# A drain on GpSimd at the start of every slot of two expert layers

## The chip, the cores and the metric

The kernel runs on one core of a Trainium2 chip. The metric is the device time of one launch in microseconds (us); the median of three runs before the change is 854.3 us (853.04 to 856.71). The core's engines are named as in the profile: PE (TensorE matmul) and PEld (its weight loads), DVE (VectorE), ACT (ScalarE), POOL (GpSimd) and SP (SyncE). A name with a q behind it (POOLq, SPq) is the engine's own instruction queue: its waits, branches, register moves and drains, which the page does not count as busy.

## The reference

Three stages follow each other: a retention attention, a top-1 expert layer, and a second top-1 expert layer whose output is gated.

```python
# attention: 4 batches, 8 heads, 768 steps, head size 64
state = gamma * state + outer(k[t], v[t])
y[t] = scale * q[t] @ state
# layer 1: x is (3072, 512), 8 experts, F = 1024
logits = x @ w_gate + modality_bias[modality_id]
e = argmax(logits); gate = softmax(logits)[e]
x = gate * (relu(x @ w1[e]) @ w2[e])
# layer 2: the same with its own weights, and one more factor
out = gate * sigmoid(x @ w_output_gate)[e] * (relu(x @ w1[e]) @ w2[e])
```

## The kernel before

The attention runs over 24 units of 128 rows. As soon as a unit's rows have their expert and their place, GpSimd writes them to a scratch tensor in HBM, sorted by expert, with an indirect DMA (`scatter`, L469: one DMA for 128 rows). 24 such DMAs carry layer 1's input (`x1d`). Each expert layer then works on *slots* of 256 rows of one expert: rows are fetched by plain DMAs from SP's queue, transposed and split in two parts by DVE and ACT, multiplied with the expert's weights on PE (three products for each, since weights and activations are split into a high and a low part), and given their gate. A slot that holds at most 128 rows takes a smaller path (`run_small`); a branch on a count decides at run time. Layer 1's slots scatter their result, one slot later, to the second scratch tensor (`x2d`, L469 again, two DMAs for a slot); layer 2's slots scatter straight to the output (`done`, L919, two DMAs for a full slot and one for a small one).

Every slot begins with `ids`: on GpSimd a handful of tiny operations on 128 by 1 or 128 by 2 elements, which mark rows that don't belong to the slot (L845 to L859). In layer 1 they make `valid` and `invalid` (L852, L854) and copy the row numbers into the output tile (L856); DVE reads them when the slot's rows are routed, in the middle of the next slot. In layer 2 they make `to` (L858, L859), the row numbers that the slot's own output DMAs use.

In layer 1's first slot GpSimd has more to do: it makes two of the four low parts of the second weight matrix (`w2l`, L511, 128 by 1024 elements each) right behind `ids`, and behind them issues the last two of the 24 scatters. In layer 2's first slot it makes two as well.

The order within an engine is that of the program; each engine runs its own list and waits for others by semaphores alone. Where two branches meet, the one that issued fewer of GpSimd's DMAs raises those DMAs' semaphores by an instruction on GpSimd's queue (INC_SWDGE_SEM in the trace), so that both sides leave the same counts. At the end of the program every engine drains and all meet at a barrier; those instructions carry the line of the launch, L1202.

Of the kernel before, what the change touches and what calls it, by code (L numbers as in the profile page):

```python
# [416 lines left out]
def retention_moe_moe_kernel(ctx: ExitStack, tc: tile.TileContext, q, k, v, mod, mb, wg, wg2, w1, w2, cst_d, out):  # L417
    nc = tc.nc
# [184 lines left out]
    with ExitStack() as actx:  # L603
# [114 lines left out]
        for t0, t1 in groups:  # L718
            g, ids = group1(t0, t1, misc)
            late.setdefault(t1, []).append(g["choose"])  # L720
            early.setdefault(t1 + 1, []).append(g["rank"])
            late.setdefault(t1 + 1, []).append(g["place"])
            late.setdefault(t1 + 1, []).append(lambda g=g, ids=ids: seq([g["weigh"], lambda: once(ids)]))
            for t in range(t0, t1):
                written.setdefault(t + 6 if t < n - 12 else t1 + 2 + (t - t0) // 2 if t < n - 8 else n - 2 + (t - n + 8) // 3, []).append(t)
# [4 lines left out]
        for i in range(n):  # L730
# [52 lines left out]
            if i == n - 4:  # L783
                fetch_rows(x1d, first_row(rp1), 2, xqf, xmf, after=scattered[-4:] + blanks)
        g1, ids = group1(n - 2, n, misc)
        ids()


    with ExitStack() as mctx:
# [28 lines left out]
        class Slot:  # L818
# [20 lines left out]
                return fetch_rows(self.src, at, 2, self.xq, self.xm, cond, after, full, **kw)  # L839

            def ids(self, full=True):

                ts = slice(self.t0, self.t0 + 2)
                if not full:
                    nc.gpsimd.memset(invalid[:, ts][:, 0:1], float(2 * E * APART))  # L845
                    if self.li == 1:
                        nc.gpsimd.memset(valid[:, ts][:, 0:1], 0.0)
                for h in range(not full, 2):
                    t = slice(self.t0 + h, self.t0 + h + 1)
                    at = self.xm[:, h, R_BIG:R_BIG + 1]  # L850
                    pl = cst[:, C_PH + h:C_PH + h + 1]
                    nc.gpsimd.tensor_scalar(invalid[:, t], at, pl, float(2 * E * APART), op0=ALU.is_gt, op1=ALU.mult)  # L852
                    if self.li == 1:
                        nc.gpsimd.tensor_scalar(valid[:, t], at, pl, None, op0=ALU.is_le)  # L854
                if self.li == 1:
                    nc.gpsimd.tensor_copy(self.o[:, :, DM + R_ID], self.xm[:, :, R_ID])  # L856
                else:
                    nc.gpsimd.tensor_tensor(invalid[:, ts], invalid[:, ts], self.xm[:, :, R_ID], op=ALU.add)  # L858
                    nc.gpsimd.tensor_copy(to[:, ts], invalid[:, ts])  # L859
# [347 lines left out]
```

## Time and profile before

| what | us |
|---|---|
| median of three runs | 854.3 |
| the profiled execution's own time | 853.39 |
| its span, from the first to the last instruction | 851.5 |
| PE busy | 799.0 |
| DVE busy | 430.3 |
| ACT busy | 276.2 |
| POOL busy | 202.1 |

Busy time counts the engines' data instructions. The profiled execution took 1.9 us more than its span (launch and end, which no instruction covers). The page's chain of waits follows data instructions back from the last one, so it begins and ends with work; what the queues do after the last data instruction stands in the views of a line's instructions, which give for every kind the count, the least, median and greatest duration in ns, and the first and last start.

### The profile page before, as it was taken

Reading aid. Unit: us, or ns where it says so; the run is one execution under the profiler, and the core shown is the slowest. Engines: PE = TensorE matmul, PEld = TensorE weight load, DVE = VectorE, ACT = ScalarE, POOL = GpSimd, SP = SyncE. Lnnn points to the kernel's source line nnn. Section 1 sums busy time; section 2 is a strip of 40 time slices with the busy share of each in tenths; the row PEclk is TensorE's granted clock in tenths of the full one; section 3 lists DMA queues with packets and bytes.
Section 4 is the critical chain, followed back from the end, with each engine's and each line's share of the span. In section 5 each row is a group of like instructions: output and inputs, shape, how many; then the busy total and the mean of one; then the engine's idle time right before and its main releaser. Section 6 shows DMA issues by size and latency. Waiting matters only on the chain. (4 is left out here: it accounts for less than half of the span.)

```text
span 851.5 us, 18413 instructions
## 1 busy us (share of the span) xinstructions
PE 799.0 (94%) x5987; PEld 696.2 (82%) x5987; DVE 430.3 (51%) x1110; ACT 276.2 (32%) x476; POOL 202.1 (24%) x291
## 2 busy tenths in 40 slices
PE   8999998799999998999999787999999999999992
PEld 7888877788889977888899576997889888888871
DVE  4554556744444338334454676144555673545921
ACT  3444445312122124121222451113252551514610
POOL 3455456712221011222210032011211112020210
PEclk9999999899999999999999999999999999999997
DMA  9987799272111015311222523412726385252610
GB/s 163 236 224 185 177 240 305 99 253 72 40 40 51 15 53 162 116 53 51 58 71 52 177 76 121 157 40 54 251 65 209 100 285 172 94 173 70 207 40 16
DMA packets 149688, 106.98 MB, mean 126 GB/s; under 512 B 94845, under 2 KB 125693, under 8 KB 149504
## 3 DMA queue, kind: packets, MB, share of 16 engines
q1 hardware_dynamic: 141664, 85.37, 37.2%
q0 software_dynamic: 6400, 18.98, 6.0%
q8 instruction: 73, 1.20, 0.6%
q14 instruction: 111, 0.91, 0.4%
q10 hardware_dynamic: 1440, 0.53, 0.3%
HBM read 167.64 MB, written 25.83 MB: 227 GB/s over the span
## 5 line engine op out<-in xcount | busy, mean ns | idle before, releaser
L891 PE MATMUL hT<-xh,w1h 128*128 128x256 f32 x768 | 222.4, 290 | 4.7 <-issue 2.9
L891 PE MATMUL hT<-xl,w1h 128*128 128x256 f32 x768 | 216.7, 282 | 1.4 <-DVE xl L547 1.4
L891 PE MATMUL hT<-xh,w1l 128*128 128x256 f32 x768 | 216.5, 282 | 0.0
L909 PE MATMUL po<-w2h,hh 128*128 128x512 f32 x432 | 172.6, 400 | 0.3
L909 PE MATMUL po<-w2l,hh 128*128 128x512 f32 x432 | 171.2, 396 | 0.0
L891 PEld LDWEIGHTS hT<-xh,w1h 128*128 128x128 f32 x768 | 146.4, 191 | 12.4 <-issue 11.0
L891 PEld LDWEIGHTS hT<-xl,w1h 128*128 128x128 f32 x768 | 146.6, 191 | 2.9 <-DVE xl L547 2.2
L891 PEld LDWEIGHTS hT<-xh,w1l 128*128 128x128 f32 x768 | 146.4, 191 | 0.0
L909 PE MATMUL po<-w2h,hl 128*128 128x512 f32 x432 | 136.3, 396 | 0.5 <-DVE hl L904 0.5
L883 DVE SCALAR_TENSOR_TENSOR hl<-hT,hh 128x512 fp32r<-128x512 f32 x96 | 65.5, 689 | 136.3 <-ACT hh L882 105.8
L882 ACT ACTIVATE hh<-hT 128x512 fp32r<-128x512 f32 x96 | 57.0, 596 | 201.7 <-PE hT L891 191.9
L909 PEld LDWEIGHTS po<-w2h,hl 128*128 128x128 f32 x432 | 81.1, 188 | 21.8 <-DVE hl L904 2.0
L909 PEld LDWEIGHTS po<-w2h,hh 128*128 128x128 f32 x432 | 81.6, 189 | 19.6 <-ACT hh L903 1.6
L909 PEld LDWEIGHTS po<-w2l,hh 128*128 128x128 f32 x432 | 81.6, 189 | 18.0
L469 POOL DMA_INDIRECT x2d<-ob,r_idx x28 | 29.6, 1059 | 261.0 <-DVE ob L260 174.5
L919 POOL DMA_INDIRECT out_dram<-ob,to x28 | 30.2, 1079 | 217.4 <-DVE ob L917 139.8
L545 ACT ACTIVATE xh<-xTb 128x512 fp32r<-128x512 f32 x58 | 33.5, 624 | 88.5 <-DVE xTb L540 79.7
L511 DVE TENSOR_TENSOR w2l<-raw,w2h 128x1024 fp32r<-128x1024 f32 x40 | 47.3, 1234 | 13.7 <-DMA xqb<-x1d 6.2
L506 DVE TENSOR_TENSOR w1l<-raw,w1h 128x512 fp32r<-128x512 f32 x80 | 49.8, 683 | 2.5 <-ACT w1h L505 2.5
L547 DVE TENSOR_TENSOR xl<-xTb,xh 128x512 fp32r<-128x512 f32 x58 | 37.6, 690 | 22.3 <-ACT xh L545 22.3
L505 ACT ACTIVATE w1h<-raw 128x512 fp32r<-128x512 f32 (+1 forms) x84 | 47.7, 640 | 0.0
L915 DVE TENSOR_SCALAR ob<-po,xmb 128x512 f32<-128x512 f32 x24 | 18.0, 750 | 54.5 <-PE po L909 54.5
(205 smaller groups left out, 997.9 us busy)
## 6 DMA issues: line engine op xcount, KB each, us to landing
raw<-in_w_dram SPq DMA_DIRECT2D x248, 512.0 KB
xqb<-x2d SPq DMA_DIRECT2D x124, 64.0 KB
xqb<-x1d SPq DMA_DIRECT2D x108, 64.0 KB
nq<-in_q_dram SPq DMA_DIRECT2D x24, 256.0 KB
nk<-in_k_dram SPq DMA_DIRECT2D x24, 256.0 KB
nv<-in_v_dram SPq DMA_DIRECT2D x24, 256.0 KB
x1d<-zrow SPq DMA_DIRECT2D x4, 516.0 KB
x2d<-zrow SPq DMA_DIRECT2D x4, 516.0 KB
```

The lines of the kernel that those rows point to most:

```text
L469: return nc.gpsimd.indirect_dma_start(out=dst, out_offset=bass.IndirectOffsetOnAxis(ap=rp.idx[:, t:t + 1], axis=0), in_=row, in_offset=Non ...
L505: nc.scalar.activation(w1h[i][:, cols], raw1[i][:, cols], AF.Copy)
L506: los[i].tensor_tensor(w1l[i][:, cols], raw1[i][:, cols], w1h[i][:, cols], op=ALU.subtract)
L511: los[i].tensor_tensor(w2l[i], raw2[i], w2h[i], op=ALU.subtract)
L545: nc.scalar.activation(hi[:, k:k + 2, :], xT[:, k:k + 2, :], AF.Copy)
L547: nc.vector.tensor_tensor(lo[:, k:k + 2, :], xT[:, k:k + 2, :], hi[:, k:k + 2, :], op=ALU.subtract)
L882: nc.scalar.activation(hh[b], hT[b], AF.Relu)
L883: nc.vector.scalar_tensor_tensor(hl[b], in0=hT[b], scalar=0.0, in1=hh[b], op0=ALU.max, op1=ALU.subtract)
L891: nc.tensor.matmul(to, lhsT=a[k][:, fs], rhs=b[:, k, :], start=(k == 0 and m == 0), stop=(k == KD - 1 and m == 2))
L909: nc.tensor.matmul(po[h], lhsT=x[b][:, o:o + P], rhs=w[f // 2][:, f % 2, :], start=(f == 0 and i == 0), stop=(f == KF - 1 and x is hl))
L915: nc.vector.tensor_scalar(perm(o[:, :DM]), plain(po[h]), gate, None, op0=ALU.mult)
L919: nc.gpsimd.indirect_dma_start(out=out, out_offset=bass.IndirectOffsetOnAxis(ap=to[:, t:t + 1], axis=0), in_=o[:, :DM], in_offset=None, bo ...
```

## The change

`ids` gets a first line: an explicit drain on GpSimd. The operations behind it, their order and the waits of all engines stay as they were; on PE, ACT, SP and POOL the two programs have the same instructions in the same order but for the drains themselves (on DVE only numbers in the names of temporary tiles differ). The built program has 81 more drains on GpSimd, since both sides of every branch hold one; an execution meets one for each slot that it runs.

```diff
             def ids(self, full=True):
+                nc.gpsimd.drain()
 
                 ts = slice(self.t0, self.t0 + 2)
                 if not full:
```

## Rows read from the trace of the kernel before

**Rows 1.** The page: the span, and busy time, share of the span and instructions of two engines.

```profile
span 851.5 us, 18413 instructions
PE 799.0 (94%) x5987; PEld 696.2 (82%) x5987; DVE 430.3 (51%) x1110; ACT 276.2 (32%) x476; POOL 202.1 (24%) x291
```

**Rows 2.** Stretches of time: start and end, length, then for each engine busy us and instructions, the granted TensorE clock, the DMA share and GB/s. The last 13 us.

```profile
core 0: us, PE busy (x) PEld busy (x) DVE busy (x) ACT busy (x) POOL busy (x), PEclk, DMA share, GB/s
838.50:851.50 13.00, 0.00 (x0) 0.00 (x0) 0.00 (x0) 0.00 (x0) 0.01 (x1) 0.54 0.06 21
```

**Rows 3.** The instructions of L1202 (the program's end) from 843 us to 850.8 us, and then the drains behind them: count, duration in ns least/median/greatest, first and last start.

```profile
L1202 SPq EVENT_SEMAPHORE  x12: 28/28/28, 843.8 to 844.5; - x12
L1202 SPq DRAIN  x2: 7/10/13, 844.6 to 844.7; - x2
L1202 POOLq DRAIN  x1: 6610/6610/6610, 844.1 to 844.1; - x1
...
L1202 POOLq DRAIN  x2: 46/78/111, 850.9 to 851.2; - x2
L1202 ACTq DRAIN  x1: 8/8/8, 850.9 to 850.9; - x1
```

**Rows 4.** The instructions of L1194 (the program's beginning) on GpSimd's queue, the same columns.

```profile
L1194 POOLq INC_SWDGE_SEM  x1: 31/31/31, 0.1 to 0.1; - x1
L1194 POOLq DRAIN  x1: 171/171/171, 0.3 to 0.3; - x1
```

**Rows 5.** Four of the later INC_SWDGE_SEM on GpSimd's queue, in order of time, from the views of the lines L1136, L1086 and L1164, the same columns.

```profile
L1136 POOLq INC_SWDGE_SEM  x1: 1272/1272/1272, 534.2 to 534.2; - x1
...
L1086 POOLq INC_SWDGE_SEM  x1: 1337/1337/1337, 597.6 to 597.6; - x1
...
L1086 POOLq INC_SWDGE_SEM  x1: 1746/1746/1746, 837.2 to 837.2; - x1
...
L1164 POOLq INC_SWDGE_SEM  x1: 1767/1767/1767, 842.1 to 842.1; - x1
```

**Rows 6.** GpSimd's groups of instructions by line and tile: count, busy us, mean ns of one, idle time before and what ended it; and for the DMAs to the output, then to `x1d`, the time from issue to landing, least/median/greatest.

```profile
L919 POOL DMA_INDIRECT out_dram<-ob,to x28 | 30.2, 1079 | 217.4 <-DVE ob L917 139.8 <-DVE hl L883 18.3 <-issue 18.1
L469 POOL DMA_INDIRECT x2d<-ob,r_idx x28 | 29.6, 1059 | 261.0 <-DVE ob L260 174.5 <-DVE w1l L506 40.7 <-issue 22.1
L469 POOL DMA_INDIRECT x1d<-yn,r_idx x24 | 24.9, 1037 | 14.6 <-DVE P L655 3.6 <-DVE r_meta L334 3.2 <-ACT yn L578 3.0
L859 POOL CAST to<-invalid 128x2 uint32<-128x2 f32 x16 | 3.0, 187 | 1.1
L856 POOL COPY ob<-xmb 128x2 f32<-128x2 f32 x13 | 2.4, 186 | 7.8 <-DMA x2d<-ob,r_idx 5.0 <-issue 2.7
L856 POOL COPY ob<-xmf 128x2 f32<-128x2 f32 x1 | 0.2, 179 | 0.0
...
DMA to landing us min/median/max: 2.7/2.9/3.1
...
DMA to landing us min/median/max: 2.8/4.5/6.0
```

**Rows 7.** GpSimd in order of time (start, us, line, operation, tiles, count, in brackets the idle time before and its releaser): a full slot of layer 1; `w2l` in layer 2's first slot; and the least idle time behind `ids` of any slot, in layer 2.

```profile
224.67 0.97 POOL L469 DMA_INDIRECT x2d<-ob,r_idx  x1 [0.30 <-issue]
225.68 0.32 POOL L852 TENSOR_SCALAR invalid<-xmb,cst 128x1 f32<-128x1 f32 x1
...
227.82 0.18 POOL L856 COPY ob<-xmb 128x2 f32<-128x2 f32 x1
247.98 1.08 POOL L469 DMA_INDIRECT x2d<-ob,r_idx  x1 [19.98 <-DVE ob L260]
...
507.04 5.80 POOL L511 TENSOR_TENSOR w2l<-raw,w2h 128x1024 fp32r<-128x1024 f32 x2 [9.07 <-ACT w2h L510]
...
793.17 1.30 POOL L919 DMA_INDIRECT out_dram<-ob,to  x1 [6.37 <-DVE hl L904]
...
796.48 0.19 POOL L859 CAST to<-invalid 128x2 uint32<-128x2 f32 x1
802.33 0.10 POOL L1066 MEMSET ob<- 128x1 f32 x1 [5.66 <-DVE ob L1064]
```

**Rows 8.** All engines in order of time, layer 1's first slot: GpSimd, and the choice of experts for the attention's last rows (DVE L190 to L207, PE L215), the columns as in rows 7; and the three runs of L190 from 130 us to 170 us, the columns as in rows 3.

```profile
161.50 4.67 POOL L511 TENSOR_TENSOR w2l<-raw,w2h 128x1024 fp32r<-128x1024 f32 x2
161.63 4.57 DVE L190 TENSOR_TENSOR rdz<-r_lg,rmx 128x16 f32<-128x16 f32 x1
166.65 0.17 DVE L207 TENSOR_TENSOR r_oh<-rq,rm 128x16 bf16<-128x16 f32 x1
166.87 0.17 PE L215 MATMUL misc<-r_oh,cb 128*128 128x16 bf16 x1 [3.98 <-DVE r_oh L207]
...
169.38 1.08 POOL L469 DMA_INDIRECT x1d<-yn,r_idx  x1 [3.22 <-DVE r_meta L334]
...
L190 DVE TENSOR_TENSOR rdz<-r_lg,rmx x3: 192/2066/4569, 134.1 to 161.6; 128x16 f32<-128x16 f32 x2, 128x32 f32<-128x32 f32 x1
```

**Rows 9.** The stretch behind PE's wait of rows 8, columns as in rows 2; and in order of time the second slot's input getting ready on DVE and PE's first weight load of that slot.

```profile
167.10:170.50 3.40, 3.40 (x17) 3.40 (x18) 2.86 (x25) 0.60 (x1) 1.08 (x1) 0.50 0.00 0
...
182.12 1.29 DVE L547 TENSOR_TENSOR xl<-xTb,xh 128x512 fp32r<-128x512 f32 x2 [0.77 <-ACT xh L545]
...
183.78 0.19 PEld L891 LDWEIGHTS hT<-xh,w1h 128*128 128x128 f32 x1
```

## The prediction

> **What bounds the kernel now.** I read the page first: PE is busy for 799.0 of 851.5 us, GpSimd for 202.1 [rows 1]. Nothing that GpSimd does inside a slot should set the time, and a change to GpSimd alone would be worth nothing were the page the whole story. It is not, for busy time leaves out the queues. The view of stretches shows 13 us at the end in which no engine works on data [rows 2], and the instructions of the program's last line say what fills half of it: a drain on GpSimd that begins at 844.1 and takes 6.610 us, after which the barrier opens at once (850.7) and the program is over at 851.5 [rows 3]. On ACT a drain takes 8 ns, on SP 7 to 13. The chain of waits doesn't show this, since it ends at the last data instruction. So the tail is set by GpSimd's queue, and that is the place that I price.
>
> **What that drain waits for.** The last output DMA was issued at about 837.4 and such DMAs land 2.7 to 3.1 us after issue [rows 6], so by 840.5, while the drain starts at 844.1. It isn't waiting for that data. Three rows say that it works off a backlog of GpSimd's DMAs. The drain at the program's beginning, with none issued yet, took 0.171 us; the two behind the long one, with nothing issued in between, took 0.111 and 0.046 us [rows 3, 4]. And INC_SWDGE_SEM, which handles the same DMAs' semaphores, grows through the run: 0.031 us with none issued, 1.272 at 534.2 us, 1.337 at 597.6, 1.746 at 837.2 and 1.767 at 842.1 [rows 4, 5]. The DMAs issued by then, counted along the time line, are 54, 58, 79 and 80 (24 + 28 + 28 in all [rows 6]): (1.767 - 1.272) / (80 - 54) = 0.019 us for each, and the two values between lie on that line within 0.02 us. Something is kept for every DMA ever issued, and no instruction before the end clears it. By that the long drain pays 6.610 / 80 = 0.083 us for each.
>
> Here a page speaks against the change: the Trainium skill, "VectorE: DVE Perf Modes", section "The DRAIN you can't avoid", says of the drains ahead of and behind a program that they are a constant 12 ns or so on all five engines. By it the added drains would cost nothing and save nothing, and the time would stay at 854.3. The rows of ACT and SP agree with it (7 to 13 ns); GpSimd's 6610 ns doesn't, and the measurement decides.
>
> **The change, part by part.** One drain is added to each slot that runs: 14 in layer 1 (13 + 1 of L856) and 16 in layer 2 (L859), 30 in all [rows 6]. Each follows the last DMA of the slot before, and what is queued behind it is `ids`.
>
> *A drain inside a slot.* Its cost is not shown before; the rows bound it by 0.046 us (nothing to do) and 6.61 us (the longest). By the backlog reading it has two DMAs to work off, 2 x 0.083 = 0.17 us, and waits until they have landed: issued at 224.67, landed 2.7 to 3.1 us later, thus about 2 us beyond 225.68, where `ids` begins now [rows 7]. I take 2.2 us. Behind `ids` GpSimd is idle for 20 us in a full slot of layer 1, and for 5.66 us in the tightest slot [rows 7]; nothing but GpSimd's own DMA (layer 2) or the next slot's routing (layer 1) waits for `ids`. So 29 of the 30 cost nothing. In layer 2's first slot it is hidden too, for `w2l` there waits 9.07 us for ACT [rows 7].
>
> *Layer 1's first slot.* Here `ids` is followed at once by `w2l`, 4.67 us on GpSimd from 161.50. DVE's L190, a 0.19 us operation elsewhere, began at 161.63 and took 4.57 us: it was held until both `w2l` were done, and PE stood still for 3.98 us behind it and then ran at the 1.2 GHz level (granted clock 0.50) for 3.4 us [rows 8, 9]. The page "SBUF — State Buffer" of the Trainium skill, section "SBUF: two separate sides", calls this an exclusive lock that goes to whichever of DVE and GpSimd starts first; the row agrees. The drain has 22 DMAs behind it (all but the last two of 24), 22 x 0.083 = 1.8 us, and moves `w2l` to about 162.4. DVE's chain from L190 to L207 needs 0.8 us undisturbed (0.6 us from the end of L190 at 166.20 to that of L207 at 166.82, and its own 0.19), so it would be through at about 162.4 as well: a toss-up. If it is through, PE is 4 us ahead, but the second slot's input hangs on DVE's place chain, which still waits for `w2l` to end, and xl is ready only 0.4 us before PE needs it now (183.41 against 183.78 [rows 9]). So PE's lead can't be used beyond about 1.3 us, and another stop and another 3.4 us at half clock (1.7 us) may eat it. If it isn't through, everything is 0.9 us later. Between -1.3 and +0.9, I take +0.3 us.
>
> *The end.* The last slot is small and issues one DMA, so the last drain finds one: 0.171 + 0.083, some 0.2 us. What is late next is SP: its 12 waits run from 843.8, when GpSimd's last INC_SWDGE_SEM is over, to 844.7 [rows 3], so the barrier can't open before about 0.85 us after that instruction; then 0.8 us as now. The end from there on is 1.65 us instead of 851.5 - 843.87 = 7.63: -5.98 us. The INC_SWDGE_SEM of 1.767 us falls to what is left without a backlog, 1.767 - 80 x 0.019 = 0.25: -1.5 us. The one at 837.2 (1.746 us) does so too, but beside the DMA of 837.4, so I count half of 1.4: -0.7 us, with both ends, 0 and -1.4, kept for the range.
>
> Sum: -5.98 - 1.5 - 0.7 + 0.3 = -7.9 us. The profiled execution took 853.39, so 845.5 us by it; the median of the runs is 0.9 us above it, and the changed kernel's time is a median too: 854.3 - 7.9 = 846.4 us.
>
> **The rivals.**
>
> *The drain clears the backlog, but INC_SWDGE_SEM counts every DMA ever issued.* For it: its growth is the only thing measured, not its fall. Then 5.98 alone is saved: 854.3 - 5.98 + 0.3 = 848.6 us.
>
> *The slots' drains clear nothing for the end* (the change doesn't do what it says): the 6.6 us are a step of the end itself, or every drain walks through all DMAs so far. For it: only one long drain was seen. Against it: 0.111 and 0.046 us right behind it. The time is 854.3 + 0.3, up to 855.2 with the first slot's 0.9.
>
> *A fixed price for any drain that finds a DMA, about 6.6 us.* Then the end keeps its drain, and the first slot pays: `w2l` ends at 161.50 + 6.6 + 4.67 = 172.8, the scatter behind it goes from 169.38 to 172.8, past its 3.22 us of idle time, the second slot's input comes 3.4 us later, 2.9 of which PE feels, and standing still that long costs 3.4 us at half clock again: 2.9 + 1.7 = 4.6, so 858.9 us, slower than before. It decides from 3.2 us of drain in this slot on. Against it: the growth of INC_SWDGE_SEM by the count.
>
> **How the numbers follow.** The forecast has a chance of 0.63, the half gain 0.12, no gain 0.16, the fixed price 0.09. What a measurement can tell from no change is 0.5%, 4.3 us. The forecast's own range goes from 854.3 - 8.6 - 1.3 = 844.4 (the whole of the 1.4, the first slot at its best) to 848.1 (none of it, the first slot at +0.9, 0.4 us for runs). Together with the half gain that holds some 7 in 10; to have 8 it reaches over the case without gain: 844.0 to 855.2. Faster by over 0.5%: 0.75, the first two cases; within 0.5%: 0.17; slower: 0.08.
>
> **What would show it.** Right: GpSimd's drain at the end under 0.5 us; 30 drains on its queue in the slots, about 2 us each, the first near 1.8; the INC_SWDGE_SEM late in the run under 0.4 us; about 5 us in place of 13 behind the last data instruction; PE's sum of waits as before but for layer 1's first slot. Wrong: a drain of several us left at the end, or slots whose PE idle time grows behind `ids`.

## The result and the profile after

The changed kernel takes 841.91 us (median of 4 runs, 840.37 to 843.6); the kernel before took 854.96 beside it (4 runs, 853.04 to 856.71). The ratio is 0.9845, with a 95% interval of 0.9816 to 0.9874: about 13 us faster. The predicted time was 846.4 us, and the measured one lies below the predicted range. Two later timings of the changed kernel, called `again` and `again_b` below, gave 0.9849 and 0.9842.

The page after, the lines that answer to [rows 1]:

```profile
span 839.4 us, 18443 instructions
PE 796.4 (95%) x5987; PEld 691.8 (82%) x5987; DVE 430.2 (51%) x1110; ACT 276.4 (33%) x476; POOL 192.5 (23%) x291
```

There are 30 instructions more, one drain for each slot, and 12.1 us less of span. PE's busy time has fallen by 2.6 us only. Most of the gain is time in which PE did nothing, and it lies in two places.

**The end.** The end of the program on the queues of GpSimd and SP from 834 us on, which answers to [rows 3] (columns as there; L1203 is the line of the end now, since one line was added). Behind it the last two INC_SWDGE_SEM, which answer to the last two of [rows 5]:

```profile
L1203 SPq EVENT_SEMAPHORE  x14: 17/28/1795, 836.0 to 839.4; - x14
L1203 POOLq DRAIN  x3: 50/111/381, 837.7 to 839.2; - x3
...
L1087 POOLq INC_SWDGE_SEM  x1: 170/170/170, 834.8 to 834.8; - x1
...
L1165 POOLq INC_SWDGE_SEM  x1: 172/172/172, 835.9 to 835.9; - x1
```

The greatest drain at the end is 0.381 us where it was 6.610, and the semaphore instructions fell from 1.746 and 1.767 to 0.170 and 0.172. What is late now is SP: one of its waits takes 1.795 us. It ends when the last output DMA has landed, as far as the profiles show: here the landing is not recorded, in `again` it is (issued at 832.27 us, landed at 835.26), and SP's wait there ends at 835.29. Before the change the landing came long before the drain was over. The stretch from PE's last product to the end, in the view of stretches (columns as in [rows 2]), before and then after:

```profile
834.79:851.50 16.71, 0.00 (x0) 0.00 (x0) 1.24 (x3) 0.00 (x0) 1.18 (x2) 0.64 0.06 19
```

```profile
832.36:839.40 7.04, 0.00 (x1) 0.00 (x0) 1.24 (x3) 0.00 (x0) 1.18 (x2) 0.77 0.13 46
```

The work of DVE and POOL in it is the same to the hundredth (1.24 and 1.18 us), and the stretch is 9.7 us shorter.

**Layer 1's first slot.** All engines in order of time after the change, where [rows 8] stood. GpSimd first, then DVE:

```profile
163.75 0.18 POOL L857 COPY ob<-xmf 128x2 f32<-128x2 f32 x1
163.90 4.75 POOL L511 TENSOR_TENSOR w2l<-raw,w2h 128x1024 fp32r<-128x1024 f32 x2
170.03 1.08 POOL L469 DMA_INDIRECT x1d<-yn,r_idx  x1 [1.38 <-DVE r_meta L334]
```

```profile
163.19 0.18 DVE L190 TENSOR_TENSOR rdz<-r_lg,rmx 128x16 f32<-128x16 f32 x1
...
163.82 0.17 DVE L207 TENSOR_TENSOR r_oh<-rq,rm 128x16 bf16<-128x16 f32 x1
...
164.95 1.38 DVE L222 COPY r_base<-rR 128x8 f32<-128x8 f32 x1
166.24 2.45 DVE L227 TENSOR_TENSOR rR<-rR,r_oh 128x16 f32<-128x16 f32 x1
```

L190 takes its 0.18 us again, L207 has begun 0.08 us before `w2l` begins, and PE has its input. The two `w2l` now hold two later operations of DVE, L222 and L227, for which PE doesn't wait at once. The view of PE's waits, before and then after (total us, times, longest):

```profile
PE misc L215 <- DVE r_oh L207: 6.0, 2, 4.0
```

```profile
PE misc L215 <- DVE r_oh L207: 2.1, 1, 2.1
```

The wait of 4.0 us is gone, and with it the half clock behind it: the stretch of [rows 9] reads so now, with a granted clock of 1.00 in place of 0.50.

```profile
167.10:170.50 3.40, 3.40 (x23) 3.08 (x23) 3.37 (x22) 0.60 (x1) 2.02 (x2) 1.00 0.02 5
```

**Elsewhere.** From one full slot of layer 1 to the next PE needs 24.75 us before (208.70 to 233.45) and 24.74 after (207.21 to 231.95), with a drain in each. Two stretches did move. Layer 1's second slot is 0.7 us longer, 25.43 us (181.78 to 207.21) against 24.69 (184.01 to 208.70), because PE now waits for input between its first two products. The first two slots of layer 2 together are 2.3 us shorter, 53.89 against 56.24; kernels without a drain there have nearly the same (`delay` 54.30, `noport` 54.50), so this isn't put down to the drains. What is left of the span, without layer 1's first two slots and the end, is 779.5 us before and 779.8 after, and lies between 776.5 and 781.5 in the twelve profiled executions below.

### The profile page after: what moved, and what is told of

It reads as the page before. It is cut to its first block, busy times and chain, and to the rows that moved or that the text cites. A ratio compares the mean times of both kernels' runs of the same rounds, so it can differ in the third digit from the quotient of the medians.

```text
span 839.4 us, 18443 instructions
## 1 busy us (share of the span) xinstructions
PE 796.4 (95%) x5987; PEld 691.8 (82%) x5987; DVE 430.2 (51%) x1110; ACT 276.4 (33%) x476; POOL 192.5 (23%) x291
## 5 line engine op out<-in xcount | busy, mean ns | idle before, releaser
L511 DVE TENSOR_TENSOR w2l<-raw,w2h 128x1024 fp32r<-128x1024 f32 x40 | 47.3, 1233 | 14.2 <-DMA xqb<-x1d 6.7
L540 DVE STREAM_TRANSPOSE xTb<-xqb 128x1024 f32<-128x1024 f32 x29 | 36.0, 1242 | 24.4 <-DMA xmb<-x2d 13.4
```

Source lines behind the costliest of these rows:

```text
L511: los[i].tensor_tensor(w2l[i], raw2[i], w2h[i], op=ALU.subtract)
L540: nc.vector.transpose(xT.rearrange("p k (a i) -> p a k i", i=32), xq.rearrange("p a (k i) -> p a k i", k=KD))
```

## The experiments

Two quantities are compared below. The *slot* is the time on PE from the first product of layer 1's first slot to the first product of the second slot. The *tail* is the time from the end of PE's last product to the end of the span. Both come from each kernel's one profiled execution; the ratios come from the timings. The kernel before had a median of 853.57 us beside the first four runs, 855.18 beside the next four and 854.67 beside the last two.

| kernel | slot | tail | ratio, 95% interval |
|---|---|---|---|
| before | 30.61 | 16.73 | 1 |
| after | 27.17 | 7.07 | 0.9845 (0.9816 to 0.9874) |
| late | 31.17 | 7.07 | 0.9891 (0.9849 to 0.9932) |
| first1 | 27.26 | 13.01 | 0.9921 (0.9897 to 0.9945) |
| first2 | 31.85 | 8.36 | 0.9905 (0.9870 to 0.9940) |
| delay | 28.62 | 14.89 | 0.9951 (0.9927 to 0.9975) |
| noport | 25.94 | 16.40 | 0.9944 (0.9920 to 0.9967) |
| again | 27.41 | 7.09 | 0.9849 (0.9823 to 0.9876) |
| dvew2l | 25.69 | 7.10 | 0.9811 (0.9774 to 0.9847) |
| dveall | 25.65 | 7.53 | 0.9829 (0.9803 to 0.9855) |
| dvew2l_b | 25.68 | 6.92 | 0.9831 (0.9791 to 0.9872) |
| again_b | 27.28 | 6.92 | 0.9842 (0.9801 to 0.9883) |

Where the first slot is short, the second gives some of it back: it takes 24.7 us in `before`, `late` and `first2`, and 25.1 to 25.5 in the nine others.

My theory after the result: two gains that have nothing to do with each other, the cleared backlog at the end and the moved `w2l` in layer 1's first slot. The rival: all of it is the backlog, and the first slot's difference is chance.

**`late`: drains only in layer 2, from its third slot on.** The first slot keeps its old order, while the end finds everything cleared.

```diff
             def ids(self, full=True):
+                if self.li == 2 and self.i >= 2:
+                    nc.gpsimd.drain()
```

> Drains only in layer 2 from its third slot on. Backlog theory: the first of these drains finds some 56 DMAs and works them off in GpSimd's idle time (56 x 0.083 = 4.6 us on its queue), the drain at the end falls to about 0.4 us and the tail behind PE's last matmul from 16.7 to about 7.0 us; nothing changes before the third slot of layer 2, so the time falls by 9.7 us alone, ratio about 0.9887. Rival, the rest of the 13 us comes with the tail as well: ratio 0.985 as with all drains. Rival, a drain clears only what was issued in its own slot: end drain near 6 us, ratio 1.00.

Measured 0.9891, which is 9.3 us. The first slot is as before: DVE is held again, this time two operations by one `w2l` each (columns as in [rows 7]), and PE waits 3.62 us behind them. The tail is 7.07 us.

```profile
163.88 4.67 POOL L511 TENSOR_TENSOR w2l<-raw,w2h 128x1024 fp32r<-128x1024 f32 x2
...
164.17 2.11 DVE L190 TENSOR_TENSOR rdz<-r_lg,rmx 128x16 f32<-128x16 f32 x1
...
169.05 0.17 PE L215 MATMUL misc<-r_oh,cb 128*128 128x16 bf16 x1 [3.62 <-DVE r_oh L207]
```

So some 9 us belong to the end alone, and they don't need a drain in every slot. The interval reaches down to 0.9849, so this time by itself doesn't exclude that the end is the whole gain; the slot in the profile and the runs that follow do. The drain at the end takes 1.815 us here and not the 0.4 that was expected: it begins 1.2 us after the last DMA's issue (838.14 against 836.92) and is over 0.05 us behind SP's wait (839.96 against 839.91). The first of the drains in the slots finds 56 DMAs (columns as in [rows 3]):

```profile
L843 POOLq DRAIN  x1: 4650/4650/4650, 564.9 to 564.9; - x1
```

**`first1`: one drain, in layer 1's first slot.**

```diff
+                if self.li == 1 and self.first:
+                    nc.gpsimd.drain()
```

> A drain only in layer 1's first slot. Backlog theory: 22 DMAs are off the list, so the drain at the end takes (80 - 22) x 0.083 = 4.8 us in place of 6.61, the last INC_SWDGE_SEM 1.767 - 22 x 0.019 = 1.35; tail 16.7 - 2.6 = 14 us. With the port theory (w2l moved behind DVE's choice of experts) the slot itself is some 3.4 us shorter on PE: together 5 to 6 us, ratio 0.993. If the 3.4 us are drift between executions: ratio 0.997.

Measured 0.9921, 6.7 us. The slot is as short as in the changed kernel (27.26). The end keeps a backlog of 58 DMAs, since the drain cleared 22 of the 80.

**`first2`: one drain, in layer 2's first slot.**

```diff
+                if self.li == 2 and self.first:
+                    nc.gpsimd.drain()
```

> A drain only in layer 2's first slot. Backlog theory: it finds 50 DMAs and takes about 50 x 0.083 = 4.2 us or a little more (landing of the last two); 30 are left for the end: 30 x 0.083 = 2.5 us, the last INC_SWDGE_SEM 0.2 + 30 x 0.019 = 0.8; the tail falls by 4.1 + 1 to 2 us. If the 4 us that this slot was shorter on PE with all drains belong to the drain, they show here too (ratio 0.989); if they are drift of instruction fetch or clock, ratio about 0.993.

Measured 0.9905, 8.1 us; the slot is as before (31.85, with a wait of 4.26 us). The drain cleared 50 DMAs, and 30 are left. It took 5.911 us, of which 50 x 0.083 are 4.15; the last packets of the DMAs ahead of it moved until 3.3 us into it. In the profiles layer 2's first slot was 4 us shorter after the change (28.26 us) than before (32.23); with a drain there it takes 28.07 to 31.07 us in seven kernels, without one 28.22 to 32.23 in five, so that difference isn't the drain's. The drains at the end and the last INC_SWDGE_SEM of `first1`, then of `first2` (columns as in [rows 3]):

```profile
L1204 POOLq DRAIN  x3: 56/111/4810, 838.0 to 843.4; - x3
...
L1166 POOLq INC_SWDGE_SEM  x1: 1317/1317/1317, 836.5 to 836.5; - x1
```

```profile
L1204 POOLq DRAIN  x3: 52/111/2507, 841.7 to 844.7; - x3
...
L1166 POOLq INC_SWDGE_SEM  x1: 752/752/752, 840.7 to 840.7; - x1
```

With the kernel before and `late` that makes four points for the drain: 6.610 us for 80 DMAs, 4.810 for 58, 4.650 for 56, 2.507 for 30, that is 0.083 or 0.084 us for each. The last INC_SWDGE_SEM goes from 1.767 to 1.317 and 0.752: (1.767 - 0.752) / 50 = 0.020 us for each. What counts is the number of DMAs since the last drain, in both.

Not every INC_SWDGE_SEM lies on that line. Four others, which carry the launch's line and which the rows and the prediction left out, took about 0.73 us before, with 50 to 53 DMAs, where the one at 534.2 us took 1.272 with 53 or 54:

```profile
L1202 POOLq INC_SWDGE_SEM  x4: 719/733/740, 508.0 to 526.6; - x4
```

After the change the same four take 0.122 to 0.131 us, so they grew with the backlog too, by 0.012 us for each DMA. Why these cost less isn't shown.

**`delay`: no drain; GpSimd is kept busy for 4 us ahead of `ids` in layer 1's first slot** by four fills of a tile that isn't used then. If the first slot gains because `w2l` comes later and not because of a drain, this gains too.

```diff
+                if self.li == 1 and self.first:
+                    for _ in range(4):
+                        nc.gpsimd.memset(hs, 0.0)
```

> No drain; instead GpSimd sets a tile of 128 x 1024 that nothing reads then to zero four times ahead of the first slot's ids in layer 1 (4 x 0.97 = 3.9 us). Port theory: w2l starts behind DVE's choice of experts, DVE's L190 takes 0.2 us and not 4.6, PE's wait of 4.0 us goes and its granted clock stays at 1.0 there; the body is about 3 us shorter, the tail is as before (end drain 6.6 us): ratio 0.996 to 0.997. Rival, the drain itself did it: ratio 1.00 and the wait stays.

Measured 0.9951, 4.2 us, and the end still has its drain of 6.610 us. GpSimd and DVE in order of time: `w2l` begins at 165.24, when DVE is past L207, and L190 is not held. The slot is 1.4 us longer than with a drain (28.62 against 27.2 to 27.4): PE waits 2.1 us for DVE's `hl` in it, where it waits 1.1 after the change.

```profile
160.02 4.01 POOL L844 MEMSET hs<- 128x1024 f32 x4
...
165.24 4.75 POOL L511 TENSOR_TENSOR w2l<-raw,w2h 128x1024 fp32r<-128x1024 f32 x2
```

```profile
163.73 0.17 DVE L190 TENSOR_TENSOR rdz<-r_lg,rmx 128x16 f32<-128x16 f32 x1
...
164.35 0.17 DVE L207 TENSOR_TENSOR r_oh<-rq,rm 128x16 bf16<-128x16 f32 x1
```

So holding GpSimd back makes this kernel faster: the gain of the first slot is one of timing, and the drain is there only a delay.

**`noport`: no drain; in layer 1's first slot DVE makes all four low parts.** The same claim from the other side: GpSimd's two `w2l` are gone.

```diff
-split2([nc.gpsimd] * 2 + [nc.vector] * 2, ...)
+split2([nc.gpsimd if self.li == 2 else nc.vector] * 2 + [nc.vector] * 2, ...)
```

> No drain; in layer 1's first slot DVE makes all four w2l and GpSimd none. Port theory: no GpSimd operation holds DVE's L190 (0.2 us), the 4 us wait of PE is gone, the slot is 27 to 28.5 us on PE; DVE has 2.5 us more work there, in time that it is idle. End drain 6.6 us as before. Ratio 0.995 to 0.996. Rival, the delay of ids itself matters and not what w2l holds: ratio 1.00.

Measured 0.9944, 4.8 us, with all of the old tail (16.40 us). The slot is 25.94 us. L190 and PE's product for it, in the views of these lines from 155 us on: no wait is left.

```profile
L190 DVE TENSOR_TENSOR rdz<-r_lg,rmx x1: 195/195/195, 162.6 to 162.6; 128x16 f32<-128x16 f32 x1
...
L215 PE MATMUL misc<-r_oh,cb x1: 169/169/169, 163.5 to 163.5; 128*128 128x16 bf16 x1
```

**`dvew2l` and `dveall`: all drains, and less work on GpSimd.** `dvew2l` is the changed kernel with the edit of `noport`. `dveall` goes further: DVE makes all of `w2l` in both first slots, and one of four low parts of the first weights in the attention.

```diff
-split1([nc.gpsimd] * KD, ...)
+split1([nc.gpsimd] * 3 + [nc.vector], ...)
-split2([nc.gpsimd] * 2 + [nc.vector] * 2, ...)
+split2([nc.vector] * 4, ...)
```

> All drains and, in layer 1's first slot, all four w2l on DVE. If what is left in that slot (1.1 us of waiting for hl, 0.7 us for xh and xl) is DVE's place chain held by w2l, the slot falls from 27.2 to about 26 us and the ratio to 0.983; if DVE's 2.5 us of added work takes their place, no change against all drains, 0.9845.

> All drains, w2l of both layers' first slots on DVE, and the last w1l of the attention too (GpSimd keeps three). By the port theory PE's 2.1 us wait at the attention's end (L190 held 2.1 us) goes or shrinks, worth 2 us and 1.7 us of half clock, and the 2.6 us wait in layer 2's first slot shrinks by the 1.3 us for which L190 is held there: ratio 0.979 to 0.982. Against it: in layer 2's first slot DVE is already late, and 2.5 us more work in its order may make that wait longer: 0.985 to 0.987.

Measured 0.9811 and 0.9829, beside 0.9849 for `again`, the changed kernel itself:

> The changed kernel itself once more, for the split between tail and body. If the whole is the tail (9.3 us by the drains of layer 2 alone) and layer 1's first slot (3.4 to 4 us): ratio 0.9845 to 0.985, tail behind PE's last matmul about 7 us, first slot of layer 1 about 27.2 us on PE against 30.6 to 31.9 in the kernels with w2l in its old place. If the body's share was drift, ratio near 0.989.

The slot is 1.6 us shorter in both, but the intervals overlap. So `dvew2l` and the changed kernel were timed once more side by side:

> The kernel with all its drains, and the four low parts of layer 1's first slot all made by DVE, timed a second time beside the changed kernel. The parts measured so far: in layer 1's first slot the changed kernel is 27.2 to 27.4 us long, the one without GpSimd's two operations 25.7, so 1.5 to 1.7 us less if nothing behind it gives that back: a ratio of 0.983 where the changed kernel has 0.985. Against: DVE has 2.4 us more work there and the end is the same, so the two ratios agree within their intervals, as they did (0.9774 to 0.9847 against 0.9823 to 0.9876).

> The changed kernel itself, as a measure beside the other: 0.985, and GpSimd's drain at the end under 0.5 us.

That gave 0.9831 and 0.9842. Both pairs point to a version 1 to 3 us faster than the changed kernel, and neither shows it: in the profiles the gain in the slot is certain, in the times it is not told apart from none.

## Why the prediction was wrong, point by point

The sign and the mechanism of the backlog were right; the sum, -7.9 us, was too small by 5 us. It had two parts, and the runs give the size of each. The end is larger by 0.7 us than I summed; the step that failed is the term of layer 1's first slot, which has the wrong sign.

**The backlog: right.** The drain of 6.610 us was 80 DMAs at 0.083 us, and the growth of INC_SWDGE_SEM was a backlog which a drain clears: `first1`, `first2` and `late` show both, with four points on one line for the drain. The rival by which INC_SWDGE_SEM counts all DMAs ever issued is out (0.172 us at the end), and so are the rival without clearing and that of a fixed price (0.229 us for a drain below). The rule of the Trainium skill ("VectorE: DVE Perf Modes", section "The DRAIN you can't avoid") of a constant 12 ns or so on all engines doesn't hold for GpSimd's drains here: 6610, 4810 and 2507 ns for 80, 58 and 30 DMAs.

**The drains in the slots: cost right, duration short.** I took 2.2 us each. The view of their line and, under it, of three stretches (columns as in [rows 3]):

```profile
L842 POOLq DRAIN  x30: 229/2652/6169, 156.8 to 822.1; - x30
...
L842 POOLq DRAIN  x1: 5717/5717/5717, 156.8 to 156.8; - x1
...
L842 POOLq DRAIN  x1: 229/229/229, 175.8 to 175.8; - x1
...
L842 POOLq DRAIN  x1: 2894/2894/2894, 223.5 to 223.5; - x1
```

The last two both have two DMAs to clear. At 175.8 these were issued some 4 and 6 us earlier, and it takes 0.229 us, that is 2 x 0.083 and 0.06 on top; at 223.5 the second of them was issued at 223.19, and it takes 2.894 us. So a drain waits for the landing, as I had assumed: where the trace has it, the drain ends 0.1 us behind (issued at 272.62, landed 2.9 us later, drain over at 275.63). It doesn't wait with the rest until then: the first drain of `late` took 4.650 us for 56 DMAs, although the packets of the last of them moved until 1.0 us into it. Where SP's transfers fill the DMA engines (80.7% of their time from 594.9 to 602.3) the landing comes later, and the drain is longer (6.169 us at 596.1). It cost nothing even there: from the slot around it to the next, PE needs 23.01 us before (592.83 to 615.84) and 23.02 after (589.84 to 612.86).

**The end: nearly right, by errors that cancelled.** I summed -5.98 - 1.5 - 0.7 = -8.2 us. With all 80 DMAs left, the tail was 16.73, 14.89 and 16.40 us, mean 16.0; with a drain in every slot, or in layer 2's from the third on, 6.92 to 7.53, mean 7.1: -8.9 us. `late`, which has this part alone, measured 9.3 us. In the two profiled executions (-9.7 us) the pieces compare so, from the issue of the last output DMA on:

| piece | before | after |
|---|---|---|
| issue of the last output DMA to the end of the INC_SWDGE_SEM ahead | 1.53 | -0.05 |
| from there to the next wait on GpSimd's queue, past a branch | 2.69 | 0.48 |
| its waits | 0.46 | 0.44 |
| the last INC_SWDGE_SEM | 1.77 | 0.17 |
| from there to the end | 7.65 | 3.37 |

The last row fell by 4.3 us, not by 5.98: I had SP's 12 waits as the next thing late, and had set the landing aside because it came early before. With everything else gone, SP waits 1.795 us for it. Against that, the INC_SWDGE_SEM ahead, of which I counted half (-0.7), stood wholly on the path (-1.6). And the piece behind it shrank by 2.2 us, which I hadn't priced at all. This piece isn't an effect of the drains alone: `delay` clears nothing and has 1.0 us between its two INC_SWDGE_SEM, where the kernel before has 3.2, `noport` 3.1, and `late` 0.9. What GpSimd's queue waits for behind that branch in some executions stays open. In the two with the longest piece, two transfers on the queue of instructions, of 8 KB each, lie in it (before from 840.01 and 840.38, `noport` from 832.70 and 832.76), in `delay` none; that GpSimd waited for them isn't shown.

**Layer 1's first slot: the step that failed.** I wrote "Between -1.3 and +0.9, I take +0.3 us". The three kernels without a drain or another delay there and with GpSimd's `w2l` have 30.61, 31.17 and 31.85 us, mean 31.2; the four with a drain 27.17, 27.26, 27.41 and 27.28, mean 27.3. The slot gained 3.9 us. The second slot gives 0.7 of it back (24.7 us in those three, 25.4 in those four), so the step is worth -3.2 us where I had +0.3 and at best -1.3. `delay` (4.2 us, interval 2.1 to 6.2) and `noport` (4.8, 2.8 to 6.8), which leave the end its backlog, bear out in the times that the gain is there without a drain. Two things in the step were off.

First, the toss-up fell to one side. I had `w2l` at 162.4, 0.9 us later than before. The working that I gave doesn't lead there: 161.50 + 22 x 0.083 = 163.3, and by that DVE's chain (162.4) would have been through with 0.9 us to spare. What takes the other 0.9 us off the prediction doesn't say. The trace has the pieces, on GpSimd before and then after:

```profile
159.12 0.12 POOL L806 MEMSET ob<- 128x2 f32 x1
...
159.77 1.36 POOL L852 TENSOR_SCALAR invalid<-xmf,cst 128x1 f32<-128x1 f32 x1
```

```profile
160.53 0.12 POOL L806 MEMSET ob<- 128x2 f32 x1
162.66 0.31 POOL L853 TENSOR_SCALAR invalid<-xmf,cst 128x1 f32<-128x1 f32 x1 [2.01 <-issue]
```

The drain is recorded from 156.8 to 162.5, 5.717 us, but for most of that GpSimd still had work of its own, scatters up to 158.6 and fills of tiles (L805, L806) up to 160.65. From the end of the fills to its own end the drain takes 1.87 us, in `again`, `again_b` and `first1` as here, and 22 x 0.083 is 1.83. So its price was right. Against it, `ids` needs 1.2 us where it needed 2.3: its second L852 took 1.36 us before, beside an operation of DVE's of 1.23 us (L511, from 159.82), and takes 0.31 after. `w2l` came at 163.90; the slot itself began 1.2 us later in that execution (154.61 against 153.40), so `w2l` moved by 1.2 us, near the 0.9. DVE got through, by 0.08 us in the changed kernel's profile, 0.09 in `again_b` and `first1`, and 2.25 in `again`: in three of four a hair, though each time on the same side.

Second, the lead of PE could be used. I held it to 1.3 us, since `xl`, the low part of the second slot's input, was ready at 183.41, only 0.4 us before PE's first load of that slot [rows 9]. But PE begins with the high part `xh`, and then needs only the first of the two operations that make `xl`. The beginning of the second slot after the change, in order of time:

```profile
179.76 1.25 DVE L540 STREAM_TRANSPOSE xTb<-xqb 128x1024 f32<-128x1024 f32 x1 [3.16 <-DMA xmb<-x1d]
181.76 1.29 DVE L547 TENSOR_TENSOR xl<-xTb,xh 128x512 fp32r<-128x512 f32 x2 [0.76 <-ACT xh L545]
```

```profile
181.78 0.38 PE L892 MATMUL hT<-xh,w1h 128*128 128x256 f32 x1 [0.38 <-ACT xh L545]
182.51 0.38 PE L892 MATMUL hT<-xl,w1h 128*128 128x256 f32 x1 [0.34 <-DVE xl L547]
```

and the same transposition before, with PE's first two products:

```profile
178.61 0.75 DVE L915 TENSOR_SCALAR ob<-po,xmf 128x512 f32<-128x512 f32 x1 [3.70 <-PE po L909]
180.10 1.25 DVE L540 STREAM_TRANSPOSE xTb<-xqb 128x1024 f32<-128x1024 f32 x1 [0.74 <-DVEq L923]
...
184.01 0.28 PE L891 MATMUL hT<-xh,w1h 128*128 128x256 f32 x1
184.13 0.28 PE L891 MATMUL hT<-xl,w1h 128*128 128x256 f32 x1
```

PE starts 0.68 us after `xh` begins on ACT (181.10 in the trace), where before it came 2.56 us after (184.01 against 181.45): 1.9 us of lead lay there. Some 0.6 us of that are lost again at once: the second product follows the first by 0.73 us, where it followed by 0.12 before, for it waits for `xl`. And the input itself came 1.6 us earlier in the slot (26.49 us after its start, before 28.05). Part of that is the chain on DVE up to L334: it was held for 3.5 us in place of 4.4. Another part is that the transposition stood on DVE behind L915, which waited for PE's late product; after the change it waits for the rows' landing instead. 1.9 + 1.6 = 3.5 us, the difference of the two slots (30.61 - 27.17 = 3.4). So I read as data-bound what was bound in part by PE itself, one step removed.

**The sum.** -8.9 at the end and -3.2 in layer 1's first two slots make -12.1 us; the medians of the three timings give -13.1, -13.8 and -13.2 us (854.96 to 841.91, 855.18 to 841.36, 854.67 to 841.51). The first of them has an interval of 10.8 to 15.7 us, so the sum lies within it, and about 1 us has no place. The single parts agree as closely: `first1` by the table should give -3.2 - (16.0 - 13.0) = -6.2 and measured -6.7; `first2` -(16.0 - 8.4) = -7.6 and measured -8.1.

The low end of the forecast's own range was added up wrongly as well: 5.98 + 1.5 + 1.4 is 8.9, and the 8.6 there comes out only with the first slot's +0.3 taken off, beside its -1.3. With 8.9 the low end is 844.1 in place of 844.4 us. The measured time lies below either.

## What to carry to other kernels

A drain on an engine that issues its own DMAs can have a length that depends on all DMAs since the last drain; where the end of a trace shows a long one on an engine that did little, clear it earlier in that engine's idle time, and then look at what the landing of the last DMA allows. And before a lead on one engine is called useless because its next input is late, look at what the input's own engine waited for: it may have been the late engine itself. A toss-up between two engines should carry both its outcomes, each at its full price, into the range.

## What was not expected of the hardware

- GpSimd's two operations of 2.4 us held DVE's L190 through both (4.57 us in the kernel before), but elsewhere one DVE operation each (2.11 us for L190 in `late`; 1.38 and 2.45 us for L222 and L227 after the change). L222 is a plain copy of 128 by 8 elements and was held as well. That one operation of GpSimd's holds one of DVE's agrees with the exclusive lock, for a whole instruction, that the Trainium skill describes ("SBUF — State Buffer", section "SBUF: two separate sides"); why L190 was held through both isn't shown.
- Four microseconds of useless work on GpSimd made the kernel 4.2 us faster (`delay`).
- The clearing of a backlog costs the same 0.083 us for each DMA in the middle of the program (56 in 4.650 us in `late`) as at its end, but is hidden there.
